# Two weight tails loaded as plain row halves, a second pair of banks for transposes, and a gate/up block moved ahead of an activation load

## The chip, the cores and the metric

The kernel runs on one core of a Trainium2 chip. The metric is device time of one execution in microseconds (us). A profiled execution gives the trace: which instruction ran on which engine and when. TensorE is called PE, its weight load PEld, VectorE DVE, ScalarE ACT, GpSimd POOL, and SyncE, which issues nearly all transfers, SP.

## The reference

The input x has 2048 rows of 576 numbers in bf16. It is layer-normalized once, and the result xn feeds two branches whose outputs are added to x:

```
xn  = layernorm(x)
A   = linear attention: q,k,v = xn @ wqkv (576 x 1728), 32 heads of 18
      phi(t) = where(t > 0, t + 1, exp(t)) + 1e-6
      kv = phi(k)^T v, z = sum phi(k);  o = phi(q) kv / (phi(q) z + 1e-6);  A = o @ wo
B   = (gelu(xn @ w_gate) * (xn @ w_up)) @ w_down      (hidden size 4608)
out = x + A + B
```

## The kernel before, in words

The 2048 rows are 16 tiles of 128 rows. Tile n is written x_n here, `("x", n)` loads tiles n and n + 1 together, and K_n and Q_n are the projections of tile n by the K and Q blocks of wqkv. The hidden size is 36 chunks of 128, called f; a gate/up unit g_f multiplies one chunk's gate and up weights with 512 rows at a time. Two chunks make a block, and a block is loaded by `load_gu(i, part)`: part 0 loads the gate weights `wg` (and, for even blocks, `wr`, the last 64 rows of both matrices for two blocks, by two loads), part 1 the up weights `wu`.

The inner size of 576 is 4 times 128 plus 64. PE works as two row tiles of 64 rows each (`LO`, rows 0 to 63, and `HI`, rows 64 to 127), which run beside each other. A unit (class `_Unit`) has a first pass `p1`, in which LO writes one bank and HI another, and a second pass `p2` with the banks exchanged; between them POOL issues an empty instruction, the "turn" (`swap`), that orders the two row tiles. The last 64 of the 576 inner rows are used once only, in `p1`: LO rows for output half 0, HI rows for half 1. For wqkv these tails lie in the tile `w_ends`, where rows 0 to 63 hold the left 288 columns of the tail and rows 64 to 127 the right 288 columns. `load_w_ends(1)` loads K's tail from ACT's queue, `load_w_ends(0)` loads Q's tail from SP's queue, each as one transfer with an outer dimension of two.

The head of the kernel (some 62 us) does everything at once: it loads x, normalizes it, transposes it, projects K for all tiles and Q for the first four, and computes the first 14 gate/up units g0 to g13 for the first 512 rows. The order of PE's work in the head is the list `line` (L493): t0, t1, K0, K1, Q0, t2, Q1, K2, Q2, t3, K3, g0, g1, g2, g3, and then K4, g4, K5, g5 and so on. A `t` is a set of ten small transposes of a tile on PE. They write banks 0 and 1 (`tp_bank`), at an offset `at` by tile, and ACT and DVE copy them out (`tp_copy`). The other tiles, and a second copy of tiles 0 and 1 (`xnU`), are transposed by DMA on SP's queue (`dma_transposes`, `xnT`). `p2` of a unit is issued after `p1` of the next. Units of the K and g kind share eight banks in four pairs; K4, K6, K8 use banks 0 and 1 in turn with others, so K6 waits until K4's phi on DVE has read them.

Everything in the head is a step with an engine, an assumed duration, a rank, a list of steps before it and an earliest time (`ready`). `in_order` (L68) lays these steps out in time and thereby fixes the order of instructions on each engine; the engines then run in that order, and wait for each other by semaphores. The order on SP is tied by the list `first_loads` (L594):

```
("xnU", 0), ("x", 4), ("xnU", 1), ("x", 6), ("gu", 1, 0), ("gu", 1, 1), ("x", 8), ("x", 10), ("xnT", 4), ("gu", 2, 0), ...
```

Ahead of the head stand the first loads (L204 to L218): x0, the K block of wqkv, x2, four quarters of the Q block, the Q tail, x3 and gate/up block 0 on SP; x1 and the K tail on ACT.

After the head PE forms the attention's sums and the rest of the gate/up units, and then, four times, 512 rows of down projection and gate/up. None of that is edited.

Of the kernel before, what the change touches and what calls it, by code (L numbers as in the profile page):

```python
# [8 lines left out]
ACT = mybir.ActivationFunctionType  # L9
ALU = mybir.AluOpType  # L10
BF16 = mybir.dt.bfloat16
# [3 lines left out]
P = 128  # L15
HP = 64
S = 2048
D = 576
# [8 lines left out]
HALF = D // 2  # L27
KT = 5
# [19 lines left out]
CENTRED = (0, 1)  # L48
# [39 lines left out]
def kernel(  # L88
# [11 lines left out]
    nc = tc.nc  # L100
# [14 lines left out]
    ps_all = psum.tile([P, 8, 512], F32, name="ps_all")  # L115
# [4 lines left out]
    LO, HI = slice(0, HP), slice(HP, P)  # L120
# [6 lines left out]
    xnT = persist.tile([P, KT, S], BF16, name="xnT")  # L127
# [25 lines left out]
    xn = apool.tile([P, NS, XW], BF16, name="xn")  # L153
    xcT = apool.tile([P, KT, len(CENTRED) * P], BF16, name="xcT")
    w_ends = apool.tile([P, 2, HALF], BF16, name="w_ends")
# [17 lines left out]
            nc.sync.dma_start(wqkv_sb[rows, 0:4, c:c + HALF], view[rows])  # L173

    def load_w_ends(which, on=nc.sync):
        c = which * D
        on.dma_start(w_ends[:, which, :], A_wqkv[512:576, c:c + D].rearrange("r (i c) -> i r c", i=2))

    def load_w_last(which, rows):
        c = slice(which * D, (which + 1) * D)  # L180
# [20 lines left out]
    def load_wd(dst, f0, f1, at):  # L201
# [22 lines left out]
    ident = const.tile([P, P], BF16, name="ident")  # L224
# [7 lines left out]
        out=bm3, in_=bm3, compare_op=ALU.is_ge, fill=0.0, base=0, pattern=[[-DH, 7], [0, DH]], channel_multiplier=1,  # L232
    )
    nc.gpsimd.affine_select(
        out=bm3, in_=bm3, compare_op=ALU.is_ge, fill=0.0, base=DH - 1, pattern=[[DH, 7], [0, DH]], channel_multiplier=-1,
# [72 lines left out]
    def step(name, engine, took, rank, after, call, ready=0.0, tail=0.0):  # L308
        steps[name] = _Step(engine, took, rank, after, call, ready, tail)
# [3 lines left out]
    def ln_half(n, h):  # L313
        if n not in ln_raw:
            ln_raw[n] = asmall.tile([P, 2, nc.vector.BN_STATS_DIM], F32, name="stats")
        nc.vector.bn_stats(out=ln_raw[n][:, h, :], in_=x_sb[:, n, h * HALF:(h + 1) * HALF])  # L316

    def act_sum(n):
        nc.scalar.activation(out=act_junk[:], in_=x_sb[:, n, 0:D], func=ACT.Copy, accum_out=act_acc[:])

    def act_mean(n):
        for out, by in ((mv[:, n, 0:1], 1.0), (act_bias, D ** -0.5)):
            nc.gpsimd.tensor_scalar(out=out[:], in0=act_acc[:], scalar1=-by / D, scalar2=None, op0=ALU.mult)

    def act_square(n):
        nc.scalar.activation(
            out=act_junk[:], in_=x_sb[:, n, 0:D], func=ACT.Square, bias=act_bias[:], scale=D ** -0.5, accum_out=mv[:, n, 1:2],
        )

    def centre(n):  # L330
        nc.vector.tensor_scalar(
            out=xn[:, n, :], in0=x_sb[:, n, :], scalar1=mv[:, n, 0:1], scalar2=None, op0=ALU.add if n else ALU.subtract,
        )

    def ln_aggr(n):
        nc.vector.bn_aggr(out=mv[:, n, :], in_=ln_raw[n][:])

    def ln_rstd(n, cnt):
        r = rstd[:, n:n + cnt]
        nc.scalar.activation(out=r, in_=mv[:, n:n + cnt, 1], func=ACT.Ln, bias=eps_ln[:], scale=1.0)  # L340
        nc.scalar.activation(out=r, in_=r, func=ACT.Exp, scale=-0.5)

    def ln_bias(n):
        nc.gpsimd.tensor_scalar(
            out=nbias[:, n:n + 1], in0=mv[:, n, 0:1], scalar1=rstd[:, n:n + 1], scalar2=-1.0, op0=ALU.mult, op1=ALU.mult,
        )
# [12 lines left out]
    def x_twin(n, cnt):  # L359
        nc.gpsimd.tensor_copy(out=x_sb[:, n:n + cnt, D:XW], in_=x_sb[:, n:n + cnt, XW - P:D])  # L360

    HEAD = 4
    def tp_bank(b):
        return ps_all[:, b, :].bitcast(BF16).rearrange("p (k t) -> p k t", t=HP)

    def transposes(n, at):
        for kt in range(KT):
            for b, rows in enumerate((LO, HI)):
                nc.tensor.transpose(tp_bank(b)[:, at + kt, :], xn[rows, n, kt * P:(kt + 1) * P], ident[rows, rows])  # L369

    def tp_copy(n, b, at):
        copy = nc.vector.tensor_copy if b else nc.scalar.copy
        t0 = n * P + b * HP
        copy(out=(xcT if n in CENTRED else xnT)[:, :, t0:t0 + HP], in_=tp_bank(b)[:, at:at + KT, :])

    def dma_transposes(n):
        nc.sync.dma_start_transpose(xnT[:, :, n * P:(n + 1) * P], xn[:, n, :])
# [1 line left out]
    X_AT = [3.35, 3.75, 6.50, 9.20]  # L379
# [3 lines left out]
    def load(name, sp, kb, rank, after, call, ready=0.0):  # L383
        step((name, "q"), "SP", sp, rank, after, call, ready=ready)
        step(name, "DMA", kb / 285, rank, [(name, "q")], lambda: None, ready=DMA_FREE, tail=1.2)
# [4 lines left out]
    for n in range(NS):  # L390
        first = 1.5 * n if n < 4 else 9.0 + 3.0 * (n - 4)
        both = n // 2 * 2
        after_x = [("x", both)] if n >= 4 else []
        x_at = X_AT[n] if n < 4 else 12.6 if n < 8 else 2.1 * both
        if n < 4:
            step(("twin", n), "POOL", 0.2, first, [], lambda n=n: x_twin(n, 1), ready=x_at)
        elif n == both:
            step(("twin", n), "POOL", 0.25, first, after_x, lambda n=n: x_twin(n, 2), ready=max(2.6 * n, 13.6))
        twin = ("twin", n if n < 4 else both)
        if n != 1:  # L400
            for h in range(2):
                step(("stats", n, h), "DVE", 0.42, first, after_x + [("raw", "K1")] * (n == 3) + [("phi", "K4")] * (n == 13), lambda n=n, h=h: ln_half(n, h), ready=x_at)
            step(("aggr", n), "DVE", 0.2, first, [("stats", n, 0), ("stats", n, 1)], lambda n=n: ln_aggr(n), tail=0.05)
        if n in CENTRED:
            if n:
                step(("sum", n), "ACT", 0.78, first - 3.0, [], lambda n=n: act_sum(n), ready=x_at)
                step(("mean", n), "POOL", 0.54, first - 3.0, [("sum", n)], lambda n=n: act_mean(n), tail=-0.27)
                step(("aggr", n), "ACT", 0.95, first + 2.0, [("mean", n), ("xnT", 1, 0)], lambda n=n: act_square(n))
            mean = ("mean", n) if n else ("aggr", n)
            step(("centre", n), "DVE", 0.45, first - 0.5, [mean, twin], lambda n=n: centre(n), tail=0.05)  # L410
        if n not in (1, 2) and n < 6:
            step(("rstd", n), "ACT", 0.46, first - 2.0 * (n == 3), [("aggr", n)], lambda n=n: ln_rstd(n, 1))
        elif n == both:
            m = min(n, 1) if n < 6 else n
            step(("rstd", n), "ACT", 0.46, first, [("aggr", m), ("aggr", m + 1)], lambda m=m: ln_rstd(m, 2))
            if n == 2:
                steps[("rstd", 1)] = _Step("none", 0.0, first, [("rstd", 2)], lambda: None, 0.0, 0.0)
        ready = [("rstd", n if n < 6 else both), twin]
        if NORM[n] == "A":
            step(("bias", n), "POOL", 0.27, first, ready[:1], lambda n=n: ln_bias(n))  # L420
            ready.append(("bias", n))
        on, took = ("ACT", 0.92) if NORM[n] == "A" else ("DVE", 0.45)
        if n < HEAD:
            late = n in CENTRED
            step(("norm", n), on, took, 2.5 if late else first, ready + [("tp", n)] * late, lambda n=n: ln_norm(n), tail=0.05)
            at = 5 * (n % 3)
            step(("tp", n), "PE", 0.2, 0, [("centre" if late else "norm", n)], lambda n=n, at=at: transposes(n, at), tail=0.15)
            for i, copied in enumerate((0.44, 0.30)):
                step(("xnT", n, i), "DVE" if i else "ACT", copied, first - 1.0, [("tp", n)], lambda n=n, i=i, at=at: tp_copy(n, i, at), tail=0.02)
            steps[("xnT", n)] = _Step("none", 0.0, first, [("xnT", n, 0), ("xnT", n, 1)], lambda: None, 0.0, 0.0)  # L430
            if late:
                load(("xnU", n), 1.25, 80, first + 2, [("norm", n)], lambda n=n: dma_transposes(n))
        else:
            step(("norm", n), on, took, first, ready, lambda n=n: ln_norm(n), tail=0.05)
            load(("xnT", n), 1.25, 80, first + 2, [("norm", n)], lambda n=n: dma_transposes(n))
# [105 lines left out]
    for name in line:  # L541
# [3 lines left out]
        kind, n = name[0], int(name[1:])  # L545
# [7 lines left out]
        if kind in "KQ":  # L553
            u.body = _Token(kind, n, head_banks if name in HEAD_T else banks)
            b = u.body.banks
# [5 lines left out]
            at = W_AT[kind]  # L561
        else:
            u.body = _Raw(n)
            b = u.body.two
# [6 lines left out]
            at = 0.0 if blk else 11.3  # L571
# [17 lines left out]
    for i in range(1, NS):  # L589
# [2 lines left out]
        step(("z", i), "DVE", 0.76, 80.0, of + ([("z", i - 1)] if i > 1 else []), lambda i=i: z_add(i))  # L592

    first_loads = [  # L594
        ("xnU", 0), ("x", 4), ("xnU", 1), ("x", 6), ("gu", 1, 0), ("gu", 1, 1), ("x", 8), ("x", 10), ("xnT", 4), ("gu", 2, 0), ("xnT", 5), ("gu", 2, 1), ("x", 12), ("gu", 3, 0), ("xnT", 6), ("gu", 3, 1), ("xnT", 7), ("x", 14), ("gu", 4, 0),
    ]
    for a, b in zip(first_loads, first_loads[1:]):
        steps[(b, "q")].after = steps[(b, "q")].after + [(a, "q")]
# [165 lines left out]
    for n in range(NS):  # L764
        late = n % TPC > 0
# [220 lines left out]
```

## Time and profile before

| what | us |
|---|---|
| median of 3 runs | 513.47 (513.35 to 513.78) |
| profiled execution | 513.59 |
| its span in the trace | 511.8 |
| PE busy | 502.4 (98%) |
| DVE, ACT, POOL busy | 230.2, 152.4, 8.9 |
| granted PE clock, every slice | 0.9 or more of full speed, mean 1.0 |

Times in the trace count from the span's start. A row of the timeline gives the start, the duration, the engine (with a q for its queue of transfers), the source line, the operation, the tile written and the tiles read, how many instructions are merged in it, and in brackets how long the engine was idle before it and what ended that. A row of waits gives the waiting engine and line, what it waited for, the total in us, how often, and the longest. The duration of a transfer's row on SP is the time to issue it; it lands later.

### The profile page before, as it was taken

The page shows a single profiled execution, that of the slowest core. Times are in us where ns is not written, and L with a number is a line of the kernel's source. Part 1 is how long each engine was busy: PE and PEld are TensorE (multiplying, and loading weights), DVE is VectorE, ACT ScalarE, POOL GpSimd, SP SyncE. Part 2 cuts the span into 40 slices and gives each one's busy share as a digit, 9 for nine tenths or more (in the row PEclk, how much of TensorE's full clock was granted, in tenths as well). Part 3 has the DMA queues.
Part 4 walks back from the last instruction along what each step waited for, and adds up shares of the span by engine and source line. Part 5 has one row for each costly group of instructions (what it writes and reads, how often), then busy time and mean ns, then how long its engine had stood idle before and what let it go on. Part 6 is the DMA issues. An engine that isn't in the chain of part 4 may idle for free.

```text
span 511.8 us, 11194 instructions
## 1 busy us (share of the span) xinstructions
PE 502.4 (98%) x4765; PEld 304.6 (60%) x4765; DVE 230.2 (45%) x478; ACT 152.4 (30%) x265; POOL 8.9 (2%) x34
## 2 busy tenths in 40 slices
PE   6989999999999999999999999999999999999997
PEld 5656776445877544445777544445777544445774
DVE  3866985776000765554000755554101655544101
ACT  4678844424100522333000523323000533222000
POOL 2110000000000000000000000000000000000000
PEclk9999999999999999999999999999999999999999
DMA  6999933995200356555000455564000464640000
GB/s 171 220 240 216 290 95 99 283 261 144 81 28 1 117 156 178 157 159 145 13 13 1 123 172 164 149 182 123 12 13 12 137 168 145 166 129 14 13 13 23
DMA packets 115455, 61.76 MB, mean 121 GB/s; under 512 B 24582, under 2 KB 115406, under 8 KB 115406
## 3 DMA queue, kind: packets, MB, share of 16 engines
q1 hardware_dynamic: 115132, 60.83, 45.2%
q8 instruction: 37, 0.61, 0.5%
q10 hardware_dynamic: 274, 0.22, 0.2%
q14 instruction: 12, 0.10, 0.1%
HBM read 53.60 MB, written 2.36 MB: 109 GB/s over the span
## 4 chain that ended last, share of the span: by engine, by line
PE 96%; DMA 3%; ACT 0%; issue 0%; SPq 0%; DVE 0%
PE ps_all L265 61%; PE ps_all L901 28%; PE ps_all L612 3%; PE ps_all L906 3%; DMA w_ends<-in_A_wqkv_dram 1%; DMA wqkv_sb<-in_A_wqkv_dram 1%; DMA wu<-in_B_w_up_dram 1%; PE ps_all L889 0%; PE ps_all L620 0%; PE ps_all L639 0%; ACT hT L489 0%; PE ps_all L841 0%; SPq L162 0%; DVE res L915 0%; PE ps_all L369 0%
## 5 line engine op out<-in xcount | busy, mean ns | idle before, releaser
L265 PE MATMUL ps_all<-xnT,wu 64*128 64x512 bf16 x1152 | 273.3, 376 | 1.1 <-DMA wu<-in_B_w_up_dram 1.1
L265 PE MATMUL ps_all<-xnT,wg 64*128 64x512 bf16 x1152 | 272.7, 376 | 0.4 <-DMA wg<-in_B_w_gate_dram 0.4
L265 PEld LDWEIGHTS <-wu 64*128 64x128 bf16 x1152 | 108.2, 94 | 68.9 <-DMA wu<-in_B_w_up_dram 1.4
L265 PEld LDWEIGHTS <-wg 64*128 64x128 bf16 x1152 | 108.2, 94 | 66.1 <-DMA wg<-in_B_w_gate_dram 0.9
L794 DVE TENSOR_TENSOR hT<-ps_all,gl 128x512 bf16<-128x512 f32 x130 | 89.8, 691 | 104.2 <-ACT gl L793 104.1
L901 PEld LDWEIGHTS <-hT 128*128 128x128 bf16 x1152 | 110.8, 98 | 30.9 <-issue 1.3
L793 ACT ACTIVATE gl<-ps_all 128x512 f32<-128x512 f32 x130 | 77.6, 597 | 164.1 <-PE ps_all L265 163.7
L915 DVE TENSOR_TENSOR res<-ps_all,x_sb 128x288 bf16<-128x288 f32 (+2 forms) x32 | 13.8, 455 | 146.3 <-PE ps_all L906 88.1
L901 PE MATMUL ps_all<-wd_a,hT 128*128 128x288 bf16 (+2 forms) x512 | 68.3, 286 | 0.0
L265 PE MATMUL ps_all<-xnT,wr 64*128 64x512 bf16 x288 | 56.6, 376 | 0.0
L901 PE MATMUL ps_all<-hT 128*128 128x288 bf16 (+2 forms) x384 | 52.4, 286 | 0.0
L815 ACT ACTIVATE gl<-ps_all 128x288 f32<-128x288 f32 x24 | 9.2, 409 | 121.4 <-PE ps_all L265 119.5
L901 PE MATMUL ps_all<-wd_m,hT 128*128 128x288 bf16 (+2 forms) x256 | 36.7, 286 | 0.0
L265 PEld LDWEIGHTS <-xnT 64*128 64x128 bf16 x504 | 28.4, 94 | 6.1 <-DMA xnT<-xn 0.5
L265 PEld LDWEIGHTS <-wr 64*128 64x128 bf16 x288 | 15.0, 94 | 16.6 <-issue 0.2
L265 PE MATMUL ps_all<-wqkv_sb,xnT 64*128 64x288 bf16 x256 | 21.2, 283 | 0.0
L906 PE MATMUL ps_all<-m_sb,pqT 128*128 128x288 bf16 (+2 forms) x128 | 20.9, 286 | 0.0
L612 PE MATMUL ps_all<-hT,xn 128*128 128x288 bf16 x128 | 16.0, 286 | 0.0
L316 DVE BATCH_NORM_STATS2 stats<-x_sb 128x6 f32<-128x288 bf16 x30 | 12.1, 442 | 7.2 <-DMA x_sb<-in_A_x_dram 7.1
L489 ACT CAST hT<-ps_all 128x1024 bf16<-128x1024 f32 x14 | 14.1, 1008 | 3.3 <-PE ps_all L265 3.2
L612 PEld LDWEIGHTS <-xn 128*128 128x128 bf16 x128 | 12.4, 98 | 3.5 <-issue 0.5
L906 PEld LDWEIGHTS <-pqT 128*128 128x128 bf16 x128 | 12.4, 98 | 3.3
(95 smaller groups left out, 246.4 us busy)
## 6 DMA issues: line engine op xcount, KB each, us to landing
wg<-in_B_w_gate_dram SPq DMA_DIRECT2D x72, 256.0 KB, 3.0
wu<-in_B_w_up_dram SPq DMA_DIRECT2D x72, 256.0 KB, 3.5
wr<-in_B_w_gate_dram SPq DMA_DIRECT2D x36, 64.0 KB, 3.3
wr<-in_B_w_up_dram SPq DMA_DIRECT2D x36, 64.0 KB, 2.9
wd_a<-in_B_w_down_dram SPq DMA_DIRECT2D x4, 576.0 KB, 7.8
out_dram<-res SPq DMA_DIRECT2D x15, 144.0 KB, 1.8
x_sb<-in_A_x_dram SPq DMA_DIRECT2D x6, 288.0 KB, 4.2
hT<-in_B_w_down_dram SPq DMA_DIRECT2D x4, 432.0 KB, 5.5
```

The costliest lines, as they stand in the source:

```text
L265: return nc.tensor.matmul(self.outs[i], lhsT=self.lhs(i, rows, kt), rhs=self.rhs(i, rows, kt), start=start, stop=stop, skip_group_check=True,)
L316: nc.vector.bn_stats(out=ln_raw[n][:, h, :], in_=x_sb[:, n, h * HALF:(h + 1) * HALF])
L489: nc.scalar.copy(out=hT[:, self.f:self.f + NF + 1:NF, :], in_=ps_all[:, self.two[0]:self.two[0] + 2, :],)
L612: nc.tensor.matmul(ps_all[:, two[hf], :HALF], lhsT=xn[:, n, kt * P:(kt + 1) * P], rhs=pk[:, n, hf * HALF:(hf + 1) * HALF], start=(n == 0), ...
L793: nc.scalar.activation(out=gl[:], in_=ps_all[:, b[0], :], func=ACT.Gelu_apprx_tanh)
L794: nc.vector.tensor_tensor(out=hT[:, GUB * k + i, :], in0=ps_all[:, b[1], :], in1=gl[:], op=ALU.mult)
L815: nc.scalar.activation(out=e[:, :HALF], in_=acc, func=ACT.Exp)
L901: nc.tensor.matmul(self.acc(hf), lhsT=hT[:, f, j * P:(j + 1) * P], rhs=wd(f)[:, self.parts[hf]], start=(f == 0 and not paired), stop=False ...
L906: nc.tensor.matmul(self.acc(hf), lhsT=pqT[:, c, self.ts], rhs=m_sb[:, c, self.parts[hf]], start=False, stop=(paired and c == 3), skip_grou ...
L915: nc.vector.tensor_tensor(out=self.res[:, hs], in0=self.acc(hf), in1=x_sb[:, self.n, hs], op=ALU.add)
```

## The change

Four things differ. `load_w_ends` makes two transfers of 64 rows and 288 columns each, one for each row half, in place of one. The transposes lose their offset, and tile 1 gets banks 2 and 3 while tiles 0, 2 and 3 use banks 0 and 1. In `first_loads`, gate/up block 2 comes ahead of `("x", 8)`, and x8, x10 and x12 move behind transposes that they led. The planner's assumed times of x8 and later, and of the copies on POOL that follow them, are 3 us later, and the statistics of tiles 12 and 13 are tied behind K5's phi in place of tile 13 alone behind K4's.

The order of PE's and of ACT's instructions is the same before and after, apart from the split load. On DVE, K4's clamp and phi and the normalization of tile 9 now come ahead of the statistics of tile 12, and K5's clamp and phi too. On SP the order from x6 on becomes: gate/up 1, gate/up 2 (wr, wr, wg, wu), xnT4, x8, xnT5, x10, wg of block 3, xnT6, wu of block 3, xnT7, x12, x14, gate/up 4, xnT8, xnT9. On POOL the copy for x6 moves behind g1's turn, and the copy for x8 behind the turns of g3 and K4.

```diff
     def load_w_ends(which, on=nc.sync):
-        c = which * D
-        on.dma_start(w_ends[:, which, :], A_wqkv[512:576, c:c + D].rearrange("r (i c) -> i r c", i=2))
+        for i, rows in enumerate((LO, HI)):
+            c = which * D + i * HALF
+            on.dma_start(w_ends[rows, which, :], A_wqkv[512:576, c:c + HALF])
...
-    def tp_bank(b):
-        return ps_all[:, b, :].bitcast(BF16).rearrange("p (k t) -> p k t", t=HP)
+    def tp_bank(n, b):
+        return ps_all[:, b + 2 * (n == 1), :].bitcast(BF16).rearrange("p (k t) -> p k t", t=HP)
...
-        x_at = X_AT[n] if n < 4 else 12.6 if n < 8 else 2.1 * both
+        x_at = X_AT[n] if n < 4 else 12.6 if n < 8 else 2.1 * both + 3.0
...
-            step(("twin", n), "POOL", 0.25, first, after_x, lambda n=n: x_twin(n, 2), ready=max(2.6 * n, 13.6))
+            step(("twin", n), "POOL", 0.25, first, after_x, lambda n=n: x_twin(n, 2), ready=max(2.6 * n + 3.0, 13.6))
...
-... [("phi", "K4")] * (n == 13) ...
+... [("phi", "K5")] * (n in (12, 13)) ...
...
     first_loads = [
-        ("xnU", 0), ("x", 4), ("xnU", 1), ("x", 6), ("gu", 1, 0), ("gu", 1, 1), ("x", 8), ("x", 10), ("xnT", 4), ("gu", 2, 0), ("xnT", 5), ("gu", 2, 1), ("x", 12), ("gu", 3, 0), ("xnT", 6), ("gu", 3, 1), ("xnT", 7), ("x", 14), ("gu", 4, 0),
+        ("xnU", 0), ("x", 4), ("xnU", 1), ("x", 6), ("gu", 1, 0), ("gu", 1, 1), ("gu", 2, 0), ("gu", 2, 1), ("xnT", 4),
+        ("x", 8), ("xnT", 5), ("x", 10), ("gu", 3, 0), ("xnT", 6), ("gu", 3, 1), ("xnT", 7), ("x", 12), ("x", 14), ("gu", 4, 0),
     ]
```

More of the change, by code (lines that the diff above doesn't have):

```diff
@@ L362, with transposes, tp_copy @@
     HEAD = 4
-    def tp_bank(b):
-        return ps_all[:, b, :].bitcast(BF16).rearrange("p (k t) -> p k t", t=HP)
-    def transposes(n, at):
+    def tp_bank(n, b):
+        return ps_all[:, b + 2 * (n == 1), :].bitcast(BF16).rearrange("p (k t) -> p k t", t=HP)
+    def transposes(n):
         for kt in range(KT):
             for b, rows in enumerate((LO, HI)):
-                nc.tensor.transpose(tp_bank(b)[:, at + kt, :], xn[rows, n, kt * P:(kt + 1) * P], ident[rows, rows])
-    def tp_copy(n, b, at):
+                nc.tensor.transpose(tp_bank(n, b)[:, kt, :], xn[rows, n, kt * P:(kt + 1) * P], ident[rows, rows])
+    def tp_copy(n, b):
         copy = nc.vector.tensor_copy if b else nc.scalar.copy
         t0 = n * P + b * HP
-        copy(out=(xcT if n in CENTRED else xnT)[:, :, t0:t0 + HP], in_=tp_bank(b)[:, at:at + KT, :])
+        copy(out=(xcT if n in CENTRED else xnT)[:, :, t0:t0 + HP], in_=tp_bank(n, b)[:, 0:KT, :])
     def dma_transposes(n):
@@ L401 @@
             for h in range(2):
-                step(("stats", n, h), "DVE", 0.42, first, after_x + [("raw", "K1")] * (n == 3) + [("phi", "K4")] * (n == 13), lambda n=n, h=h: ln_half(n, h), ready=x_at)
+                step(("stats", n, h), "DVE", 0.42, first, after_x + [("raw", "K1")] * (n == 3) + [("phi", "K5")] * (n in (12, 13)), lambda n=n, h=h: ln_half(n, h), ready=x_at)
             step(("aggr", n), "DVE", 0.2, first, [("stats", n, 0), ("stats", n, 1)], lambda n=n: ln_aggr(n), tail=0.05)
@@ L425 @@
             step(("norm", n), on, took, 2.5 if late else first, ready + [("tp", n)] * late, lambda n=n: ln_norm(n), tail=0.05)
-            at = 5 * (n % 3)
-            step(("tp", n), "PE", 0.2, 0, [("centre" if late else "norm", n)], lambda n=n, at=at: transposes(n, at), tail=0.15)
+            step(("tp", n), "PE", 0.2, 0, [("centre" if late else "norm", n)], lambda n=n: transposes(n), tail=0.15)
             for i, copied in enumerate((0.44, 0.30)):
-                step(("xnT", n, i), "DVE" if i else "ACT", copied, first - 1.0, [("tp", n)], lambda n=n, i=i, at=at: tp_copy(n, i, at), tail=0.02)
+                step(("xnT", n, i), "DVE" if i else "ACT", copied, first - 1.0, [("tp", n)], lambda n=n, i=i: tp_copy(n, i), tail=0.02)
             steps[("xnT", n)] = _Step("none", 0.0, first, [("xnT", n, 0), ("xnT", n, 1)], lambda: None, 0.0, 0.0)
```

## The prediction

> **What bounds the kernel now.** I read the engine totals first, then who waited on TensorE, then the DMA share while it waited, then the SP queue in order.
>
> ```profile
> PE 502.4 (98%) x4765; PEld 304.6 (60%) x4765; DVE 230.2 (45%) x478; ACT 152.4 (30%) x265; POOL 8.9 (2%) x34
> ```
>
> PE is busy for 98% of the 511.8 us span. An edit that leaves its instructions alone can only win back its gaps. The whole list of PE's waits, over the whole span:
>
> ```profile
> PE ps_all L265 <- DMA w_ends<-in_A_wqkv_dram: 3.8, 2, 2.8
> PE ps_all L265 <- DMA wu<-in_B_w_up_dram: 1.1, 1, 1.1
> PE ps_all L243 <- DVE x_sb L208: 1.1, 1, 1.1
> PE ps_all L265 <- DMA wg<-in_B_w_gate_dram: 0.4, 1, 0.4
> PE ps_all L369 <- ACT xcT L374: 0.2, 1, 0.2
> ```
>
> The first two groups and the fourth are what the change can touch: 2.83 + 0.92 us on w_ends, 1.11 + 0.40 us on gate/up block 2, together 5.26 us. The timeline of PE places them:
>
> ```profile
> 9.46 0.30 PE L265 MATMUL ps_all<-w_ends,xcT 64*128 64x288 bf16 x2 [2.83 <-DMA w_ends<-in_A_wqkv_dram]
> 12.27 0.30 PE L265 MATMUL ps_all<-w_ends,xcT 64*128 64x288 bf16 x2 [0.92 <-DMA w_ends<-in_A_wqkv_dram]
> 18.11 0.39 PE L265 MATMUL ps_all<-xnT,wr 64*128 64x512 bf16 x2
> 27.93 0.39 PE L265 MATMUL ps_all<-xnT,wg 64*128 64x512 bf16 x1 [0.40 <-DMA wg<-in_B_w_gate_dram]
> 29.43 0.39 PE L265 MATMUL ps_all<-xnT,wu 64*128 64x512 bf16 x1 [1.11 <-DMA wu<-in_B_w_up_dram]
> ```
>
> The row at 18.11 is g0, the first gate/up unit. From 12.27 to it PE runs almost without a gap. After 29.43 it waits for nothing to the end, so what is won in the head moves the end one for one. The DMA line for 8.4 to 11.4 us (0.075 us a digit) shows why w_ends is late:
>
> ```profile
> DMA  2599579699652111101111111111111546964213
> ```
>
> From about 9.3 to 10.7 only about a tenth of the sixteen DMA engines works, two of them, while PE is about to wait for the Q ends, issued at 5.93. The SP queue:
>
> ```profile
> 2.28 2.71 SPq L173 DMA_DIRECT2D wqkv_sb<-in_A_wqkv_dram  x4
> 5.93 0.64 SPq L177 DMA_DIRECT2D w_ends<-in_A_wqkv_dram  x1
> 6.62 1.29 SPq L162 DMA_DIRECT2D x_sb<-in_A_x_dram  x1
> 9.43 0.52 SPq L195 DMA_DIRECT2D wr<-in_B_w_gate_dram  x1
> 14.64 1.21 SPq L377 DMA_TRANSPOSE xnT<-xn  x1
> 24.86 0.57 SPq L199 DMA_DIRECT2D wu<-in_B_w_up_dram  x1
> ```
>
> SP stands still from 7.91 to 9.43. The built program gives every SP and ACT load one of eight completion semaphores in turn, and a load waits until the previous holder of its semaphore has landed. The first wr load shares one with the K ends, so it too waits for the two-engine load. xnU1 (14.64) carries the second tile's transposed rows for g0.
>
> **Part 1, the ends as two plain loads each.** It adds one issue on ACT and one on SP. ACT's extra issue, 0.4 to 0.6 us (the x issue there took 0.39, the ends 1.12), ends by about 2.8, before ACT's first arithmetic at 3.64: nothing. The semaphores also shift by two: the fourth Q quarter now waits for the K block, and x3 for x2; before, both waited for loads long done.
>
> K block: landed 5.92 at the latest. By the per-microsecond bandwidth (15, 263, 249, 388 GB/s from 1 us on) the 0.96 MB of x0, x1, K block and K ends had been moved by about 5.15, so it lands between 5.15 and 5.92 once no engine carries extra packets; I take 5.6, rather nearer the observed row. SP then issues: quarter 5.6, halves of Q ends 6.25 and 6.85 (0.6 each, as the quarters), x3 at 7.45. The second half lands 2.35 (x0, 0.81 to 3.16) to 3.5 us (the 64 KB wr rows) after 6.85: 9.2 to 10.35, and I take 9.9, nearer wr since quarters lie ahead of it. PE would be there earlier: unhindered, K0 starts by 5.96, needs 0.49 for its eight matmuls, and from the K ends to the Q ends PE worked 9.46 to 11.35, so 8.35. The 2.83 wait goes, a wait of about 1.5 us on Q stays, and PE is 12.27 - 9.9 = 2.4 us early.
>
> Next late is xnU1. From x3 to it SP issues x3 0.57, wr 0.52 and 0.60, wg 0.59, wu 0.57, xnU0 1.33, x4 0.57, with seven gaps of 0.065: 5.2 us. It starts at 7.45 + 5.2 = 12.65 and lands at 16.1 with its present delay (14.64 to g0's start at 18.11, 3.47). PE would arrive at 15.7. So g0 starts 18.11 - 16.1 = **2.0 us** early. Bounds: if x2 still lands at its present 8.26, x3 waits for it, xnU1 comes at 16.9, gain 1.2; if the K block lands at 5.15 and xnU1 takes 2.4 us like x0, PE's own 3.5 us would hold. The x3 data lands by 7.45 + 3.5 = 11; its statistics follow the DVE copies at 14.06 - 2.4 = 11.7, so it stays covered.
>
> The Trainium skill, page "DMA: Bandwidth & Descriptors", section "Rules for kernel authors", speaks against this edit: two transfers to disjoint partition halves serialize on the same engines, so one transfer is to be used. By that rule alone nothing would land earlier, part 1 would be worth 0 and the sum would be 512.0. The same section says that an outermost dimension under 16 confines a transfer to that many engines, which is what the one-tenth row above shows here, so I go by the row.
>
> **Part 2, own banks for the second transposes.** It removes the 0.23 us that PE waited at 5.61 for ACT's copy. PE then waits for the Q ends anyway: **0**, covered by the 1.5 us left there; without that cover a gain of at most 0.23. Banks 2 and 3 are next written by Q0 after 7, when both copies (to 6.37) are done.
>
> **Part 3, block 2 ahead of x8.** From xnU1 at 12.65: 1.21, x6 0.59, gate/up 1 0.47 + 0.51, wr 0.59 twice, wg 0.59, with gaps: the last load (wu2) is issued at about 17.6 in place of 24.86 and lands 4.51 later (its present delay), 22.1. Unit g4 asks at 27.15 - 2.0 = 25.15: the whole **1.5 us** goes; to lose it the landing would have to take 7.5 us.
>
> What it moves back: xnT4 starts at 18.2 (19.85 before) and lands 3.9 later, 22.1, against K4 at 25.67 - 2.0. x8 goes from 17.6 to about 19.5, x10 from 18.1 to about 21.95, since xnT5 stands before it on SP and waits for ACT's normalization (its end 22.68 - 2.0) and takes 1.22. On POOL the x8 copy stands before the turn of g4 (needed at about 26.2); x8 lands 4.2 (median) to 6.5 us (longest early x load) on, 23.7 to 26.0: free. On DVE the statistics of tiles 10 and 11 (1.93) stand before K4's clamp and phi (1.17), and phi frees the banks of K6. x10 lands at 26.15, phi ends at 29.25, K6 is due at 33.62 - 3.5 = 30.1: free by 0.85; with 6.5 us it ends at 31.55 and costs 1.4. I take 0 (the median row). The edit also takes x12's statistics, on which DVE stood 2.36 us, from before K4's phi: idle there cost PE nothing. xnT8 would land at 35.2 against K8 at 36.2.
>
> **Sum.** 2.0 + 0 + 1.5 = 3.5 us. The profiled execution took 513.59 (span 511.8 and 1.8 around it), 0.12 above the median of 513.47: 510.1 against itself, 510.0 against the median.
>
> **Rivals.** (1) Everything goes: xnU1 is quicker, PE keeps 3.5 us, 5.0 in all: 508.5. For it, the DMA engines are nearly idle from 9.3 to 10.7; against it, the 3.47 us of xnU1 itself. (2) Part of it: x2 late (1.2 in place of 2.0) or x10 late (1.4 lost), or both; gain 1.3 to 2.7: 510.8 to 512.2. (3) The halves land no earlier and only part 3 works: 512.0; the idle engines speak against it. (4) Slower: x10's statistics stop K4's phi on DVE, and K6 behind it. It decides once K6 starts 1.03 us later than its present 33.62, so x10 must land after 31.5, over 9.5 us after its issue, where 6.5 is the longest seen; at 11 us it gives 516.
>
> **How the numbers follow.** A measurement tells about 0.2% (1.03 us) from no change. Main case (gain 2.8 to 4.2) 0.58; rival 1 0.14; rivals 2 and 3 together 0.20; no change, two of these losses at once, 0.04; rival 4 0.04. Faster is the first three, 0.92. The range runs from 508.4 (rival 1 and the 0.23 of part 2 within it) to 512.0: it holds the main case, rival 1 and most of 2.
>
> **What would show it.** Right: PE's first wait on w_ends gone and one of 1 to 2 us left near 10; g0 near 16, released by the xnT transfer; no wait on wg or wu near 25; K6 without a wait on DVE. Wrong: a w_ends wait near 12 still; SP standing at x3 for x2 until 8.3; x10 landing after 27, with a PE wait on phi near 30.

## The result, and the profile after

The changed kernel took 511.35 us (median of 5 runs, 510.98 to 511.67) against 513.46 for the kernel before: a ratio of 0.9958, 95% interval 0.9943 to 0.9972. The gain is 2.1 us. It has the forecast sign and the time lies in the forecast range, but the forecast gain was 3.5, so 1.4 us of it are missing.

The profiled execution took 511.67, with a span of 509.9 us. Its engine totals, from the page:

```profile
PE 503.7 (99%) x4765; PEld 304.2 (60%) x4765; DVE 229.8 (45%) x478; ACT 152.2 (30%) x265; POOL 8.8 (2%) x34
```

PE's whole list of waits (total in us, times, longest):

```profile
PE ps_all L266 <- DMA w_ends<-in_A_wqkv_dram: 2.0, 2, 1.6
PE ps_all L244 <- DVE x_sb L209: 1.1, 1, 1.1
PE ps_all L266 <- DMA xnT<-xn: 0.4, 1, 0.4
```

The first wait on `w_ends` (2.83 us, at the K ends, that is K's tail in `w_ends`) is gone, and both waits on gate/up block 2 are gone. The waits on `w_ends` that are left are both on the Q ends, 0.42 us for the first half and 1.62 for the second, and a new wait on a transposed tile has appeared. The timeline of PE places them:

```profile
10.83 0.28 PE L266 MATMUL ps_all<-w_ends,xcT 64*128 64x288 bf16 x1 [1.62 <-DMA w_ends<-in_A_wqkv_dram]
...
12.39 1.35 PE L266 MATMUL ps_all<-wqkv_sb,xcT 64*128 64x288 bf16 x8
...
18.00 0.40 PE L266 MATMUL ps_all<-xnT,wr 64*128 64x512 bf16 x2
...
26.87 0.40 PE L266 MATMUL ps_all<-xnT,wr 64*128 64x512 bf16 x2
...
38.12 0.67 PE L266 MATMUL ps_all<-wqkv_sb,xnT 64*128 64x288 bf16 x8 [0.37 <-DMA xnT<-xn]
```

The second half of the Q ends is there at 10.83 and not at 12.27, so PE is 1.44 us early at this point. At g0 (18.00, before 18.11) only 0.11 of it is left. The row at 12.39 says where it went: its matmuls are those that elsewhere in the head take 0.67 us for eight, and they took 1.35. The same trace in windows (length, busy time and instructions of PE, PEld, DVE, ACT, POOL, then the granted PE clock, the DMA share and GB/s):

```profile
8.50:11.50 3.00, 0.96 (x20) 0.72 (x19) 0.46 (x2) 0.30 (x1) 0.22 (x1) 1.00 0.44 112
12.00:13.00 1.00, 1.00 (x12) 0.82 (x10) 1.00 (x4) 0.19 (x1) 0.00 (x0) 0.50 1.09 322
...
15.50:18.00 2.50, 2.47 (x48) 2.10 (x45) 1.87 (x4) 1.11 (x3) 0.30 (x1) 1.00 1.07 249
```

The granted clock is 0.50 in the middle row, as in the two microseconds after it, and PE is busy without a gap there. In finer windows the stretch runs from 11.8 to 15.2 us: it begins one microsecond after the wait and lasts 3.4 us. Half of 3.4 us is 0.33% of the span, and the mean clock of this execution is 0.997; so a mean of 0.997 fits one such stretch, and 0.993 fits two. The profile of before, with waits of 2.83 and 0.92 us at the same place, shows no such stretch:

```profile
12.00:13.00 1.00, 0.73 (x19) 0.68 (x20) 0.00 (x0) 0.00 (x0) 0.24 (x1) 1.00 0.73 209
```

The Trainium skill, page "TensorE: Matmul & The Clock Gate", section "Part 1: The HAM clock gate", speaks of a clock halved after idle windows of some 3.4 us that run freely and make the outcome vary from run to run. The halving and its variation agree with the runs here; the waits ahead of it, 2.0 us in all, are less than such a window.

SP's queue (start, time to issue):

```profile
6.19 1.25 SPq L178 DMA_DIRECT2D w_ends<-in_A_wqkv_dram  x2
...
8.12 0.48 SPq L196 DMA_DIRECT2D wr<-in_B_w_gate_dram  x1
8.64 1.31 SPq L197 DMA_DIRECT2D wr<-in_B_w_up_dram  x1
...
13.32 1.21 SPq L378 DMA_TRANSPOSE xnT<-xn  x1
...
34.45 2.54 SPq L378 DMA_TRANSPOSE xnT<-xn  x2
```

The DMA line for 8.4 to 11.4 us, which before was a row of ones and twos from 9.3 to 10.7:

```profile
DMA  4339795277899866454220110000000275551123
```

SP issues the Q ends at 6.19 and 6.84 and x3 at 7.48, within 0.06 of the forecast. The second wr load then takes 1.31 us where the first took 0.48, and xnU1 starts at 13.32 and not at 12.65. The two-engine stretch is gone from the DMA line; it falls to ones and zeros at about 10.0 and stands at zero from 10.2 to 10.7. Later, xnT8 (34.45) lands after K8 asks for it: 0.37 us.

Gram, the first work after the head, starts at 60.72, before at 62.50. Of these 1.78 us, 0.11 is there at g0; 0.17 comes between g0 and g4 (9.04 us before, 8.87 after), and 1.85 at block 2 (g4 to g5 took 4.90 us before and 3.05 after, a little more than the two waits' 1.51); 0.37 is lost at K8.

### The profile page after: what moved, and what is told of

Its sections match the earlier page's. It is cut to its first block, busy times and chain, and to the rows that moved or that the text cites. A ratio compares the mean times of both kernels' runs of the same rounds, so it can differ in the third digit from the quotient of the medians.

```text
span 509.9 us, 11195 instructions
## 1 busy us (share of the span) xinstructions
PE 503.7 (99%) x4765; PEld 304.2 (60%) x4765; DVE 229.8 (45%) x478; ACT 152.2 (30%) x265; POOL 8.8 (2%) x34
## 4 chain that ended last, share of the span: by engine, by line
PE 97%; DMA 2%; SPq 0%; issue 0%; DVE 0%
PE ps_all L266 61%; PE ps_all L902 28%; PE ps_all L613 3%; PE ps_all L907 3%; DMA wqkv_sb<-in_A_wqkv_dram 1%; DMA w_ends<-in_A_wqkv_dram 1%; DMA xnT<-xn 1%; PE ps_all L890 0%; PE ps_all L621 0%; PE ps_all L640 0%; PE ps_all L842 0%; SPq L178 0%; SPq L173 0%; SPq L162 0%; PE ps_all L370 0%
## 5 line engine op out<-in xcount | busy, mean ns | idle before, releaser
L266 PE MATMUL ps_all<-xnT,wr 64*128 64x512 bf16 x288 | 54.8, 376 | 0.0
L266 PEld LDWEIGHTS <-xnT 64*128 64x128 bf16 x504 | 26.2, 95 | 8.6 <-DMA xnT<-xn 0.7
L266 PE MATMUL ps_all<-wqkv_sb,xnT 64*128 64x288 bf16 x256 | 19.9, 288 | 0.4 <-DMA xnT<-xn 0.4
```

Of the source, the lines that this page charges most:

```text
L266: return nc.tensor.matmul(self.outs[i], lhsT=self.lhs(i, rows, kt), rhs=self.rhs(i, rows, kt), start=start, stop=stop, skip_group_check=True,)
```

## The experiments

The first theory was that the half clock took what part 1 had won: the **clock theory**. Its rival was the **supply theory**: PE at full clock would only have waited, because SP issues too late what PE asks for next. It was first written down for what stands behind g0 (block 2, and the transposes at K4 to K8); the runs below gave it its later form: SP issues xnU1 late, and g0 cannot start before xnU1 lands. Each ratio is to runs of the kernel before on the same chip.

**Part 1 alone, and part 3 alone.** The first keeps the two plain loads and the old order of `first_loads`, banks and planner times; the second keeps the old loads and banks.

```diff
+        for i, rows in enumerate((LO, HI)):
+            c = which * D + i * HALF
+            on.dma_start(w_ends[rows, which, :], A_wqkv[512:576, c:c + HALF])
```

```diff
+        ("xnU", 0), ("x", 4), ("xnU", 1), ("x", 6), ("gu", 1, 0), ("gu", 1, 1), ("gu", 2, 0), ("gu", 2, 1), ("xnT", 4),
+        ("x", 8), ("xnT", 5), ("x", 10), ("gu", 3, 0), ("xnT", 6), ("gu", 3, 1), ("xnT", 7), ("x", 12), ("x", 14), ("gu", 4, 0),
```

> Part 1 alone: the kernel before with the two plain loads for the K and the Q ends. Clock theory (the changed kernel loses most of what PE wins at the Q ends because its clock is granted at half speed from about 11.7 to 15.3 us, after PE stood idle for the Q ends): PE resumes near 10.8, some executions show the slow clock, g0 starts near 18.0 with it and near 16.7 without. Supply theory (a gain ahead of g0 does not reach the end, because the transfers that PE asks for next come when SP issues them): the wait on gate/up block 2 near 28 to 29 grows by what the head wins, since that load stands on SP behind xnT5; time 513.0 to 513.5. The prediction's part 1 by itself (2.0 us that reach the end): 511.5.

> Part 3 alone: the kernel before with the new order of loads and the new planner times, its ends and its banks untouched. The prediction's part 3: the wait on block 2 (1.51 us) goes and nothing comes in its place, 512.0. Supply theory: w_ends waits of 2.83 and 0.92 as before, block 2's wait gone, and a wait on the transpose of tile 8 at K8 of up to 0.4 us: 512.0 to 512.4. Rival: x8 and x10, issued later, hold up more than that and the gain is under 1 us.

Part 1 alone: 512.23 against 513.22, ratio 0.9978 (0.9967 to 0.9989), 1.0 us. Part 3 alone: 512.02, ratio 0.9978 (0.9966 to 0.9989), 1.2 us. Together 2.2, which agrees with the whole change's 2.1 (each of the two is uncertain by some 0.6). PE's timeline with part 1 alone:

```profile
16.29 0.39 PE L266 MATMUL ps_all<-xnT,wr 64*128 64x512 bf16 x2 [0.87 <-DMA xnT<-xn]
...
27.01 0.39 PE L266 MATMUL ps_all<-xnT,wu 64*128 64x512 bf16 x1 [1.11 <-DMA wu<-in_B_w_up_dram]
```

In this execution the clock stayed full, the Q ends were complete by about 9.6, and g0 started at 16.29, the forecast's 16.1 within 0.2. The wait on block 2 (1.11 us, before 1.11 and 0.40) has not grown, so the first form of the supply theory falls. But its time, 511.20, was the lowest of twelve. The eight executions at a mean clock of 1.0 have a median of 511.96, and the three of before on this chip at 1.0 took 512.38 to 512.93: also at full clock most executions do not show the 2.0 us. PE's timeline with part 3 alone, and its windows:

```profile
9.49 0.42 PE L265 MATMUL ps_all<-w_ends,xcT 64*128 64x288 bf16 x2 [2.71 <-DVE xn L354]
...
18.48 0.40 PE L265 MATMUL ps_all<-xnT,wr 64*128 64x512 bf16 x2
```

```profile
10.00:11.00 1.00, 1.00 (x12) 0.75 (x10) 0.00 (x0) 0.00 (x0) 0.00 (x0) 0.50 0.27 74
```

Here the clock is halved too, from 9.4 to 12.8 us, at the end of a wait of 2.71 us. It is the wait at the K ends that the kernel before also has (2.83). The row names a normalization on DVE that ended at the same time, but SP's first wr load, which waits for the K ends, starts at 9.46, as it does at 9.43 in the kernel before. g0 starts at 18.48. So the half clock is no property of part 1. Nor is it, by the mean clocks, one of the changed kernel: of 23 executions of before on this chip only three have a mean of 1.0, and five have 0.993.

**Keeping PE busy, first try.** To test the clock theory, 40 matmuls on a tile of zeros were put ahead of Q0, as a step of their own in the plan; the outputs do not use them.

```diff
+        if name == "Q0":
+            pe("warm2", 1.76, [("xnT", 0, 0), ("xnT", 0, 1)], lambda: row_spin(20, 0))
```

> The changed kernel with 40 small matmuls on a block of zeros (1.76 us) on PE ahead of Q0's first pass, into banks 0 and 1, so that PE is not idle while the Q ends travel. Clock theory: granted clock 1.0 throughout, PE goes on from 10.8 at full speed, g0 starts at 16.6 to 16.8 in place of 18.0, and the time falls by as much, to 510.0. Supply theory: g0 starts as early, but the wait on the transpose at K8 (0.37 us in the changed kernel) grows by about 0.8, and the time is 510.8 to 511.1.

It took 516.29, ratio 1.0051 (1.0034 to 1.0068), and tests something else than was meant: the planner laid out the other engines anew around the new step. DVE took the statistics of tile 4 ahead of the normalization of tile 3, waited for x4, and PE waited for DVE at the transposes of tile 3:

```profile
PE ps_all L370 <- DVE xn L355: 4.9, 1, 4.9
```

Up to that wait the clock was full; during it, at 18.8, it was halved, and stayed so until 25.6. What follows is only that one reordering on DVE makes PE wait 4.9 us, with the half clock on top.

**K and Q ends in one load per row half.** Both tails come from ACT's queue, two loads in all, and SP's two loads for Q go.

```diff
-    def load_w_ends(which, on=nc.sync):
+    def load_w_ends(on):
+        both = A_wqkv[512:576, 0:2 * D].rearrange("r (w c) -> r w c", w=2)
         for i, rows in enumerate((LO, HI)):
-            c = which * D + i * HALF
-            on.dma_start(w_ends[rows, which, :], A_wqkv[512:576, c:c + HALF])
+            on.dma_start(w_ends[rows, :, :], both[:, :, i * HALF:(i + 1) * HALF])
...
-    load_w_ends(1, nc.scalar)
+    load_w_ends(nc.scalar)
...
-    load_w_ends(0)
```

> The changed kernel with the K and the Q ends in one load per row half, both from ACT's queue: the Q ends arrive with the K ends, SP issues two loads fewer (1.25 us), and x3 no longer waits for x2. Both theories: no wait on w_ends, no half clock, xnU1 issued at about 12.0 and landed at 15.4, g0 near 15.5. Clock theory (nothing else binds): 2.5 us less than the changed kernel, 508.9. Supply theory: most of it is lost to transposes at K4 to K8, 510 to 511.

> The kernel with K and Q ends in one load per row half on ACT's queue, again, beside the two others on one chip. Expected: ratio 0.992 as before (0.990 to 0.993), g0 near 15.3 after a wait of some 0.8 us for xnU1, and a wait of 0.2 to 0.5 us at K6 for K4's phi.

509.10, ratio 0.9918 (0.9904 to 0.9932), and on another chip 509.11, ratio 0.992 (0.9901 to 0.9939): by the ratios 1.4 to 2.1 us less than the changed kernel in its two measurements (0.9958 above, 0.9947 below). PE's timeline and SP's:

```profile
15.32 0.39 PE L265 MATMUL ps_all<-xnT,wr 64*128 64x512 bf16 x2 [0.81 <-DMA xnT<-xn]
...
29.38 0.67 PE L265 MATMUL ps_all<-wqkv_sb,xnT 64*128 64x288 bf16 x8 [0.29 <-DVE hT L473]
```

```profile
6.28 0.60 SPq L162 DMA_DIRECT2D x_sb<-in_A_x_dram  x1
...
12.21 1.21 SPq L377 DMA_TRANSPOSE xnT<-xn  x1
```

No wait for the Q ends, no half clock in any of its eleven executions (mean clock 0.999 or 1.0), and no long issue at wr (xnU0's took 2.12 us, where 1.34 is usual). The clock theory had forecast 508.9, and the supply theory in its first form 510 to 511, from late transposes at K4 to K8, which did not come. But xnU1 too is issued early here, at 12.21, and PE waits 0.81 us for it. So the run does not tell the clock from xnU1; the next two do.

**The changed kernel once more, and PE kept busy without touching the plan.** Now 80 matmuls on zeros stand inside Q0's first pass, so that the plan sees the same step.

```diff
             u.p1 = u.body.unit.rows
+            if name == "Q0":
+                u.p1 = lambda body=u.body: (row_spin(40, 0), body.unit.rows())
```

> The changed kernel once more, beside the next three on one chip, so that they can be set against it. Expected from its first timing: ratio to before 0.996 (some 511.3 us where before takes 513.4). If the second half of the Q ends always lands as late as 10.8 us, the profile shows the wait of 1.6 us on it again; the run with part 1 alone saw 9.2, so any value between may come. The clock theory says: wherever PE idles about 2 us there, half clock follows within 1 us, and g0 starts near 18.0; wherever the half lands by about 9.5, the clock stays full and g0 starts near 16.2 to 16.5.

> The changed kernel with 80 extra matmuls on a tile of zeros inside Q0's first pass, ahead of its own, into banks 0 and 1 which the pass then starts anew; the order on all engines stays. By the earlier run with 40 of them (1.1 us) they take 2.2 us, 7.85 to 10.05, and Q0's own eight 0.5, so PE reaches the Q ends at about 10.5 without a gap. Clock theory: the granted clock stays at 1.0 in the head, g0 starts at 16.5 (the Q ends at 10.8 plus the 5.8 us that PE needs from there), and the time is 1.3 to 1.5 us below the changed kernel's, 509.8 to 510.1; in executions where the half lands early the extra work costs up to 1 us of this. Supply theory (g0's start was set by something else that the head lacks): g0 stays near 18.0 and the time at 511.3, or above by the extra work.

The changed kernel again: 510.56 against 513.02, ratio 0.9947 (0.9933 to 0.9961). Its clock was full in all six executions. PE and SP in its profile:

```profile
10.51 0.28 PE L266 MATMUL ps_all<-w_ends,xcT 64*128 64x288 bf16 x1 [1.16 <-DMA w_ends<-in_A_wqkv_dram]
...
17.39 0.39 PE L266 MATMUL ps_all<-xnT,wr 64*128 64x512 bf16 x2 [1.04 <-DMA xnT<-xn]
...
31.29 0.67 PE L266 MATMUL ps_all<-wqkv_sb,xnT 64*128 64x288 bf16 x8 [0.24 <-DVE hT L474]
```

```profile
8.15 1.59 SPq L196 DMA_DIRECT2D wr<-in_B_w_gate_dram  x1
...
13.74 1.21 SPq L378 DMA_TRANSPOSE xnT<-xn  x1
```

PE waits 1.16 us for the second half of the Q ends, runs on at full speed, and then waits 1.04 us for xnU1. With PE kept busy:

```profile
7.81 2.42 PE L250 MATMUL ps_all<-warm 64*128 64x128 bf16 x80
...
18.07 0.39 PE L266 MATMUL ps_all<-xnT,wr 64*128 64x512 bf16 x2 [1.67 <-DMA xnT<-xn]
```

```profile
13.74 2.17 SPq L378 DMA_TRANSPOSE xnT<-xn  x1
```

The clock was full in all twelve executions and the waits on the ends were gone, yet g0 started at 18.07, after 1.67 us of waiting for xnU1, and the time was 512.26, ratio 0.998 (0.9967 to 0.9994), worse than without the extra matmuls (g0 comes 0.7 us later, and the wait at K6 is 0.70 and not 0.24). With PE busy and the clock full, g0 still waits for xnU1, so the clock theory falls as the account of the missing gain. On the same chip, the six executions of the kernel before that had a mean clock of 1.0 have a median of 512.54, so at full clock on both sides the change is worth 2.0 us, and 1.5 of the forecast 3.5 are still missing. The half clock does cost something in the executions that have it. Of the first five runs of the changed kernel, the two with a mean clock of 0.997 took 511.49 and 511.67, the three at 1.0 took 510.98 to 511.35: some 0.5 us. Why xnU1's own issue took 2.17 us in the last profile, where 1.21 is usual, is not shown.

**Part 2 undone.** The changed kernel with all four transposes in banks 0 and 1 again.

```diff
-        return ps_all[:, b + 2 * (n == 1), :].bitcast(BF16).rearrange("p (k t) -> p k t", t=HP)
+        return ps_all[:, b, :].bitcast(BF16).rearrange("p (k t) -> p k t", t=HP)
```

> The changed kernel with part 2 undone: all four transposes write banks 0 and 1 at offsets again. By the prediction part 2 is worth nothing while a wait for the Q ends follows: a wait of 0.2 us at the second transposes comes back, the wait on the ends shrinks by as much, time within 0.2 us of the changed kernel. Rival: the wait passes through to the end, 0.2 to 0.3 us slower. The two are near each other for the times; the profile's PE rows up to the Q ends tell them apart.

510.87, ratio 0.9953 (0.9941 to 0.9966), beside 510.56 with part 2; the spreads overlap. PE's timeline:

```profile
6.11 0.67 PE L266 MATMUL ps_all<-wqkv_sb,xcT 64*128 64x288 bf16 x8
...
17.04 0.39 PE L266 MATMUL ps_all<-xnT,wr 64*128 64x512 bf16 x2 [0.30 <-DMA xnT<-xn]
```

The second transposes start 0.96 us after the first (5.01 to 5.97), where the changed kernel needs 0.50 (5.11 to 5.61), so K0 starts at 6.11 and not at 5.97. Then PE waits 1.62 us for the second half of the Q ends, as the changed kernel did in its first profile, and again at g0. Part 2's 0.14 us end in these waits, as forecast.

**Place or number of loads.** The Q ends as the changed kernel loads them, but issued on ACT's queue behind the K ends.

```diff
     load_w_ends(1, nc.scalar)
+    load_w_ends(0, nc.scalar)
...
-    load_w_ends(0)
```

> The changed kernel with its two loads of the Q ends issued on ACT's queue behind those of the K ends, not on SP's behind the quarters; the transfers themselves are the changed kernel's. SP then issues x3 at about 6.2 and all that follows 1.25 us sooner. Place theory: what part 1 still lacked is the place of the Q ends (wait of 1.2 to 1.6 us for them) and the place of xnU1 on SP (13.3 to 13.7, against a forecast 12.65); both are won here as in the kernel with both ends in one load per half, so the time is its 509.1 (ratio 0.992), PE waits under 0.5 us on the ends, g0 near 15.3 to 15.6, and the clock stays full. Rival: folding K and Q into one load was needed, since two more issues of some 0.6 us on ACT end near 4 us, behind its first arithmetic at 3.6, and delay the first tile by up to 0.8 us: 509.9 or more.

510.61, ratio 0.9949 (0.9933 to 0.9964), no better than the changed kernel, and 1.5 us behind the folded loads (509.11) on the same chip. SP and PE:

```profile
2.28 5.14 SPq L173 DMA_DIRECT2D wqkv_sb<-in_A_wqkv_dram  x4
...
8.11 1.79 SPq L196 DMA_DIRECT2D wr<-in_B_w_gate_dram  x1
...
13.89 1.21 SPq L378 DMA_TRANSPOSE xnT<-xn  x1
```

```profile
17.54 0.39 PE L266 MATMUL ps_all<-xnT,wr 64*128 64x512 bf16 x2 [2.12 <-DMA xnT<-xn]
```

The wait on the ends is gone, but SP won nothing: the four quarters take until 7.42, x3 starts at 7.46 as in the changed kernel, wr takes 1.79 us, and PE waits 2.12 us for xnU1. The built program says why. The eight completion semaphores go round over ACT's and SP's loads together, so the load that stands eight behind the K block waits for the K block to land, at about 5.5, and all of SP behind it. In the changed kernel that is the fourth quarter. Here, with two more loads of ACT's ahead, it is the second, and three quarters are issued after 5.5. The place theory falls. ACT's first arithmetic came only 0.13 us later (4.01, in the changed kernel 3.88), so the rival's price was not it either. In the folded kernel the load that waits for the K block is the fourth quarter, as in the changed kernel, and x3 follows it at once (6.28 in place of 7.48). So the folded loads take two issues off SP without adding two loads to the round.

**Fewer loads still.** The folded kernel with the Q block as one load, as the K block is, in place of four quarters: the same bytes.

```diff
-    load_w_quarters(0, (0, 1))
-    load_w_quarters(0, (1, 0))
+    load_w_main(0)
```

> The kernel with K and Q ends in one load per row half on ACT's queue, and now the Q block of wqkv as one load in place of four quarters: three issues of some 0.65 us and three loads fewer ahead of x3, with the same bytes. There x3 is issued at 6.3 behind the quarters, which take 2.27 to 6.24, and g0 waits 0.8 us for xnU1. Theory that the number of loads (their issues and their turns among the eight completion semaphores) sets the head: x3 is issued by about 4.5, xnU1 up to 0.7 us sooner (it then stands for the normalization of tile 1), the wait before g0 goes, 508.3 to 508.5. Rival 1: the transfers' bytes set it, the DMA engines being over 0.9 busy up to 9 us: x3, wr, wg and wu then move beside the Q block, which lands later, PE waits for it at Q0 (near 7.9) and the time is 509.1 to 510. Rival 2: issues that take 1.2 to 1.8 us in place of 0.6, as at wr in the changed kernel, come back ahead of xnU0, since SP runs further ahead of the engines: 509.1.

508.28 against 513.72, ratio 0.9892 (0.9874 to 0.9910), the best of all the runs; the interval overlaps that of the folded kernel a little (0.9904 to 0.9932). SP and PE:

```profile
2.95 0.69 SPq L162 DMA_DIRECT2D x_sb<-in_A_x_dram  x1
3.69 0.64 SPq L196 DMA_DIRECT2D wr<-in_B_w_gate_dram  x1
5.82 0.47 SPq L197 DMA_DIRECT2D wr<-in_B_w_up_dram  x1
...
9.64 1.20 SPq L376 DMA_TRANSPOSE xnT<-xn  x1
```

```profile
8.68 0.67 PE L264 MATMUL ps_all<-wqkv_sb,xcT 64*128 64x288 bf16 x8 [0.17 <-DMA wqkv_sb<-in_A_wqkv_dram]
...
14.85 0.40 PE L264 MATMUL ps_all<-xnT,wr 64*128 64x512 bf16 x2
```

x3 is issued at 2.95 and xnU1 at 9.64, and g0 starts at 14.85 without a wait. PE pays 0.17 us at 8.68 for the block that now comes as a whole. Eight loads behind the K block stands now the second wr load, and SP is idle from 4.33 to 5.82 before it; x3 and the first wr load are already out.

**Two shifts in the folded kernel.** The first puts xnU1 ahead of x4; the second ties the statistics of tiles 10 and 11 behind K4's phi.

```diff
-        ("xnU", 0), ("x", 4), ("xnU", 1), ("x", 6),
+        ("xnU", 0), ("xnU", 1), ("x", 4), ("x", 6),
```

```diff
-[("phi", "K5")] * (n in (12, 13))
+[("phi", "K4")] * (n in (10, 11)) + [("phi", "K5")] * (n in (12, 13))
```

> The kernel with K and Q ends in one load per row half, both on ACT's queue, and now the second tile's transposed rows (xnU1) ahead of x4 on SP. There g0 waits 0.81 us for xnU1 (issued 12.21, landed 15.3). xnU1 is issued 0.67 us earlier and x4 1.25 us later. If xnU1 alone sets g0: wait 0.15 left, time 0.6 us less, 508.4. Rival: x4's statistics come 1.2 us later, the normalization of tile 4 and xnT4 with them, and K4 waits, so that the gain is lost: 509.1 or up to 509.8.

> The same kernel with the statistics of tiles 10 and 11 tied behind K4's phi on DVE. In its profile K6 waits 0.29 us for K4's phi, which stands behind these statistics (1.93 us) and they behind x8's landing; in three profiles of the changed kernel that wait was 0.24 to 0.70. By that account the wait goes and the time is 0.2 to 0.4 us less, 508.8 (a difference the times can hardly show, the list of PE's waits can). Rival: the planner then also moves the normalization of a later tile behind, xnT of that tile comes late, and a wait on a transposed tile or on DVE further on takes its place: 509.1 to 510.

xnU1 first: 509.94, ratio 0.9946 (0.9926 to 0.9966). g0 starts at 14.52, 0.8 us sooner and without a wait, and then:

```profile
16.56 0.66 PE L265 MATMUL ps_all<-wqkv_sb,xnT 64*128 64x288 bf16 x8 [0.78 <-POOLq L276]
18.56 0.39 PE L265 MATMUL ps_all<-xnT,wr 64*128 64x512 bf16 x2 [1.34 <-DVE hT L473]
```

```profile
16.48 0.82 DVE L316 BATCH_NORM_STATS2 stats<-x_sb 128x6 f32<-128x288 bf16 x2 [2.71 <-DMA x_sb<-in_A_x_dram]
...
17.75 0.76 DVE L473 SCALAR_TENSOR_TENSOR hT<-ps_all,phi_e 128x576 bf16<-128x576 f32 x1
```

DVE stands 2.71 us for x4, with the phi at 17.75 queued behind x4's statistics, and on POOL the turn of K3 stands behind x4's copy, so that K3's second pass waits. PE pays 0.78 and 1.34 us. K4 first: 510.28, ratio 0.994 (0.9923 to 0.9958). The wait at K6 went as meant, and another came:

```profile
42.63 0.67 PE L265 MATMUL ps_all<-wqkv_sb,xnT 64*128 64x288 bf16 x8 [1.06 <-DMA xnT<-xn]
```

K10 waits for its transposed tile. The plan had moved later statistics and normalizations too; which of them is behind this wait was not separated. Both are the rivals as written down: an order that is tuned to some landing times gives back what is taken from one place.

## Why the prediction was right or wrong

**K block, Q ends, x3: right.** The K block landed at 5.53 (forecast 5.6), the halves were issued at 6.19 and 6.84 (6.25, 6.85), x3 at 7.48 (7.45), and x2 did not hold it. The first `w_ends` wait went. The second half of the Q ends was forecast between 9.2 and 10.35; PE had it at about 9.6 (part 1 alone: its two matmuls on the ends took 0.67 us from 9.19), 10.51, 10.83 and 10.90 (banks shared). So the upper bound, an issue-to-landing time of 3.5 us, was too small by about half a microsecond: 3.94 in the profiled execution. The rule that the prediction cites from the Trainium skill (page "DMA: Bandwidth & Descriptors", section "Rules for kernel authors"), against two transfers to disjoint partition halves, would have made part 1 worth 0; it was worth 1.0 (0.6 to 1.7).

**From x3 to xnU1 in 5.2 us: the step that failed.** It was worked out from issue durations and gaps of 0.065 and allowed for no long issue. The profile of before had two in this very stretch: x3's row, which the prediction shows, took 1.29 us, and the row of wu in block 0 took 1.20:

```profile
11.27 1.20 SPq L199 DMA_DIRECT2D wu<-in_B_w_up_dram  x1
```

The sum put 0.57 for each. With the changed loads these two were short, but one of the wr loads took 1.31 to 1.71 us where its like take 0.5 to 0.6, and the stretch measured 5.84, 6.22 and 6.22 us in three profiles of these loads, and 5.29 with part 1 alone. xnU1 therefore came at 12.94 to 13.74 and not 12.65. Its delay from issue to g0's start, forecast 3.47, measured 3.35, 3.50 and 3.65 where PE stood waiting for it at full clock. So g0 started between 16.3 and 17.4 in those three and at 18.0 where the half clock came on top. Of the forecast 2.0 us, the times of part 1 alone show 1.0 (0.6 to 1.7), under the lower bound of 1.2 though not clear of it. Why these issues are long stays open. The half clock was not in the prediction at all.

**Part 2: 0, right**, with the cover named: the wait for the Q ends.

**Part 3: the wait of 1.5 us went, right, but not free.** Block 2's last load was issued at 18.09 (forecast 17.6) and no unit waits for it. Against the 0 that was taken for x10 and the margin of 1.0 us for xnT8 stand waits of 0.24, 0.42 and 0.70 us at K6 for K4's phi in three later profiles, and 0.37 at K8 for xnT8 in the first one, landing at 38.08 against a forecast 35.2. Their size is in the lower half of the 0 to 1.4 named for x10, and the mechanism is nearly the one named: statistics stand ahead of K4's phi on DVE. But the load that DVE stood for was x8, not x10. The folded kernel, with 0.29 us at K6, shows it:

```profile
24.45 0.82 DVE L316 BATCH_NORM_STATS2 stats<-x_sb 128x6 f32<-128x288 bf16 x2 [3.47 <-DMA x_sb<-in_A_x_dram]
...
28.57 0.76 DVE L473 SCALAR_TENSOR_TENSOR hT<-ps_all,phi_e 128x576 bf16<-128x576 f32 x1
```

From 24.45 on the statistics of tiles 8 to 11 run without a gap, some 3.8 us, and then clamp and phi. In the three profiles with waits of 0.24, 0.70 and 0.42 the first row starts at 26.36, 27.50 and 26.38. The prediction looked at x8 for POOL's copy only and put its statistics on DVE at nothing. With them (1.93 us for each two tiles) its own latest landing of x8, 26.0, leads to a phi that ends at 31.0, where K6 was due at 30.1. Part 3 alone measured 1.2 (0.6 to 1.7), which does not exclude the forecast 1.5; its own profile lists neither wait.

**The rivals.** The main case, a gain of 2.8 to 4.2 with a chance of 0.58, did not come. Rival 2, a gain of 1.3 to 2.7 from a partial loss, is what came in size, but by another door, and that it lies in the range is luck to that extent: not x2 holding x3, but wr holding what stands behind x3. Rival 4, the slower one, showed its mechanism in small at K6, with x8 for x10, and a like one when x4 was moved.

## What to carry to other kernels

Where loads share a few completion semaphores in turn, look for the load that takes its turn behind a slow early one, and count what is queued behind it: two loads fewer won 1.4 to 2.1 us here, three more won another 0.8 (by the ratios, on different chips, 1.4), and moving two to another queue won nothing. The Trainium skill, page "DMA: Bandwidth & Descriptors", section "Rules for kernel authors", says to coalesce many small transfers into a large one, and these runs agree: 36 KB loads folded to 72 KB, and then quarters of 144 KB to one of 576 KB, both came out faster. An issue time read from a quiet part of a queue is a lower bound in a busy one. And when a kernel's order is planned around landing times, a load moved by a microsecond moves the in-order work of DVE and POOL with it; look at who is queued behind the first consumer of the load that goes back.

## What the runs showed that was not expected

The granted clock fell to 0.50 for 3.4 us within about 1 us of the end of a PE wait, in some executions and not in others: after waits of 0.42 and 1.62 us in the profile of the changed kernel and at the end of 2.71 us in that of part 3 alone, but not after 2.83 us in the profile of before. During the wait of 4.9 us it fell for 6.8 us. It cost the changed kernel some 0.5 us where it came. By the mean clock the kernel before, part 1 alone, the shared banks and the Q ends on ACT have it in some executions too. The kernels whose waits on the ends are short or gone (PE kept busy inside Q0, folded loads, Q block as one load) ran at a mean clock of 0.999 or 1.0 in all executions, though PE kept busy inside Q0 waits 1.67 us at g0. Two of six executions with xnU1 first, which waits 0.78 and 1.34 us, had 0.996 and took 511.81 and 512.20 where the other four took 509.41 to 510.21. What decides between the executions is not shown.

A load's issue on SP took 1.2 to 1.8 us at times in place of 0.5 to 0.6. It is not the same load each time (in the changed kernel the second wr load in one profile and the first in another; in the kernel before x3 and wu). In the profiled execution the second wr load's semaphore was that of the first Q quarter, whose data PE was multiplying by 8.5, and the issue ended only at 9.95; where a semaphore holds SP, as at 4.33 to 5.82 above, the queue shows idle time before the row and not a long row. In both profiles of the changed kernel the long issue ends 0.1 to 0.3 us after the DMA line has fallen to twos or less (9.95 after 9.8, and 9.74 after 9.5). That a backlog of earlier transfers holds the issue would fit, but was only argued; what is waited for stays open.

While PE waited for the second half of the Q ends, the DMA line of the changed kernel stands at zero from 10.2 to 10.7, and PE's row starts at 10.83. What passes between the last packets and the wait's end is not shown.
